# Loading routing probabilities chunk by chunk, and a small DMA in place of matmuls for the total decay

## The chip, the cores and the metric

The kernel runs on one core of one Trainium2 chip. The metric is the device time of one execution in microseconds (us). Three timed runs of the kernel before gave 314.59, 313.70 and 313.29 us, a median of 313.7 us. The engines of the core are PE (matmuls; PEld is its weight loads), DVE, ACT, POOL and SP. SP computes nothing here: it issues the DMAs, one after the other, each once what it waits for is there. POOL also issues DMAs, those of the expert weights.

## The reference

Two stages follow one another. The first is a gated recurrence for each batch and head (4 batches, 8 heads, 768 steps, head width 48), the second a mixture of 4 experts on the recurrence's output, seen as 3072 rows of 384.

```python
f = 1.0 / (1.0 + np.exp(-f_logit))
for t in range(S):
    state = f[:, :, t, :, None] * state + np.einsum('bhd,bhe->bhde', k[:, :, t], v[:, :, t])
    y[:, :, t] = np.einsum('bhd,bhde->bhe', q[:, :, t], state)
...
p = domain_probs / (domain_probs.sum(-1, keepdims=True) + 1e-09)
for e in range(E):
    h = np.maximum(x @ w1[e], 0.0)
    out += p[:, e:e + 1] * (h @ w2[e])
```

## The kernel before, in words

**Chunks.** The 768 steps are cut into 6 chunks c of 128 steps, which lie on the partitions. For each chunk and batch b the attention part works as follows. `gate1` and `gate2` (ACT, L240 and L244) turn the gate logits into -log f, called gp. `pe_cs` (PE) sums gp over the steps with a triangular matrix Ub (L248); four further matmuls (L251), one for each pair of heads, multiply gp by a column of ones, which gives the sum over the whole chunk, already on the partitions of the state (channel d of head 2i at partition d, of head 2i+1 at partition 64+d). `exps` (ACT) makes e[:,0] = exp(-sum) and e[:,1] = exp(sum) (L255, L256) and, from the four columns, egs, the total decay of the chunk (L258). `product` (L261, POOL or DVE) multiplies q by e[:,0] and k by e[:,1]. In chunks 0 and 1 PE transposes the products (L269) and ACT or DVE copies them out; from chunk 2 on a DMA does it (`dma_tp`, L273). `pe_at`, `ev_at` and `pe_y` (L284, L288, L295, L299) make the chunk's output; its transposed copy xT comes from PE in chunks 0 and 1 and from a DMA (`dma_xt`, L277) afterwards. `pe_kv`, `ev_kv` and `state` (L305, L312, L319, L320) bring the state forward: state, on POOL, multiplies it by egs and makes a bf16 copy for the next chunk. The last chunk has no state step, and so no egs.

**Experts.** For each chunk and expert e, `mm_h` (L328) multiplies xT by w1 in 8 groups of 3 matmuls; `relu` moves them out of PSUM (ACT L336, DVE L334). `mm_o` (L340) multiplies by w2, two groups of 4 matmuls for each batch nt; `ev_o` scales the result by the probability pn and adds it up in a tile o (expert 0: ACT L349 or DVE L351; experts 1 to 3: DVE L347). `store` (L355) writes o out. The relu of a later expert and the ev_o of an earlier one share ACT and DVE, each of which works in its own fixed order. PSUM has 4 banks for these results (`ps_m`), and PE can't begin a group before a bank is free.

**The probabilities.** One DMA on SP (L370) loads all 3072 rows of 4 probabilities into pt, 128 partitions by 24 columns by 4, behind the 16 loads of chunk 0. `probs` (DVE, L234 to L237) normalizes all of them once, into pn. Every `ev_o` depends on it.

**What sets the order.** A planner in the kernel, class `Plan`, gives every step a cost on the engines that may run it, a priority, what it depends on, and rooms (buffers) that it takes and frees. It plays the program through and puts the steps down in the order in which they would start; the instructions of each engine stand in that order and are waited for in that order. On SP too: a DMA whose source isn't ready holds up all those behind it. The planner's costs only set the order; the times in this document are from the chip. The weights come by 8 DMAs on POOL's queue (L229), and SP's first load of chunk 1 (f, L222) is made to wait until the sixth of them has landed. The tile e has 2 rooms, o has 8.

**Warming up.** Before the first expert matmul the program fills PE's gaps with matmuls on a tile called busy (L533).

Of the kernel before, what the change touches and what calls it, by code (L numbers as in the profile page):

```python
# [10 lines left out]
AF = mybir.ActivationFunctionType  # L11
ALU = mybir.AluOpType
# [87 lines left out]
def kernel(  # L100
# [14 lines left out]
    T = 128  # L115
# [17 lines left out]
    ps = ctx.enter_context(tc.tile_pool(name="ps", bufs=1, space=PS))  # L133
    rooms = {"ps_m": 4, "ps_t": 4, "f": 4, "q": 4, "k": 4, "v": 4, "ex": 2, "gp": 4, "e": 2, "qk": 7,
             "vb": 7, "egs": 8, "QK": 2, "AT": 2, "yb": 2, "xT": 2, "h": 2, "o": 8}
    P = Plan(rooms)
# [95 lines left out]

    def probs(eng):
        nc.vector.tensor_reduce(out=psm, in_=pt, axis=mybir.AxisListType.X, op=ALU.add)  # L234
        nc.vector.tensor_single_scalar(out=psm, in_=psm, scalar=1e-9, op=ALU.add)
        nc.vector.reciprocal(out=psm, in_=psm)  # L236
        nc.vector.tensor_tensor(out=pn, in0=pt, in1=psm.broadcast_to([128, B * C, E]), op=ALU.mult)  # L237

# [7 lines left out]
    def pe_cs(c, b):  # L246
        g, cs = tl("gp", c, b // 2)[:, b % 2], tl("cs", c, b)
        nc.tensor.matmul(out=cs[:, 0:HD], lhsT=Ub, rhs=g[:, :, 0:D], start=True, stop=True)  # L248
        if c < C - 1:
            for i in range(NP):  # L250
                nc.tensor.matmul(out=cs[0:MP, HD + i:HD + i + 1], lhsT=flat(g, i)[:, 0:MP], rhs=ones, start=True, stop=True)  # L251

    def exps(c, b):
        cs, e = tl("cs", c, b), tl("e", c, b)
        nc.scalar.activation(out=e[:, 0], in_=cs[:, 0:HD], func=AF.Exp, scale=-1.0)  # L255
        nc.scalar.activation(out=e[:, 1], in_=cs[:, 0:HD], func=AF.Exp)  # L256
        if c < C - 1:
            nc.scalar.activation(out=tl("egs", c, b), in_=cs[0:MP, HD:HD + NP], func=AF.Exp, scale=-1.0)  # L258

    def product(c, b, j, eng):  # L260
        engines[eng].tensor_tensor(out=tl("qk", c, b)[:, j, :, 0:D], in0=tl("qk"[j], c, b // 2)[:, hh(b), :],  # L261
                                   in1=tl("e", c, b)[:, j].rearrange("t (h d) -> t h d", d=D), op=ALU.mult)

# [104 lines left out]
    for i, x in enumerate("f0 k0 q0 f1 k1 q1 f2 f3 k2 q2 v0 k3 q3 v1 v2 v3".split()):  # L368
        add_load(0, x[0], int(x[1]), 1, -1000 + i)
    pload = P.add("ld p", {"DMA": 0.3}, lambda e: nc.sync.dma_start(  # L370
        out=pt, in_=moe_domain_probs.rearrange("(n p) e -> p n e", p=128)), -900, lag=2.0)
    wd = {}
# [11 lines left out]
    def attention(c, slot, gran):  # L384
        G, X, Y = {}, [], []
        more = c < C - 1
# [8 lines left out]
        for b in range(B):  # L395
# [4 lines left out]
            one = lambda f, *x: (lambda e, b=b: f(c, b, *x, e))  # L400
            cs = P.add(f"cs {c}.{b}", {"PE": 0.36 if more else 0.17}, on(pe_cs), s(0),
                       deps=[G[b]], takes=[pt_("cs")], lag=0.2, frees=[("gp", c, half)])
            ex = P.add(f"exps {c}.{b}", {"ACT": 1.1}, on(exps), s(0) + 0.1, deps=[cs],
                       takes=[("e", c, b)] + ([("egs", c, b)] if more else []), frees=[pt_("cs")])
            pe = {"DVE": 0.6, "POOL": 1.0} if c < 2 else {"POOL": 1.0}
# [61 lines left out]
    def add_o(c, e, nt, half):  # L467
# [5 lines left out]
        if half == 1:  # L473
            ev = oev[c, e, nt] = P.add(f"ev_o {c}.{e}.{nt}", {"ACT": 0.58, "DVE": 0.56} if e == 0 else {"DVE": 0.62},
                                       lambda g: ev_o(c, e, nt, g), p - 1, deps=[m, oev.get((c, e - 1, nt)), pdone],
                                       takes=[("o", c, nt)], frees=[key])
# [4 lines left out]
    pdone = P.add("probs", {"DVE": 1.2}, probs, 3, deps=[pload, xdone[0, B - 1]])  # L481
    ALL, LO, HI = list(range(B)), [0, 1], [2, 3]
# [13 lines left out]
    def ol(c, e, nts):  # L496
        return [(c, e, nt, half) for nt in nts for half in range(2)]

    for c in range(C):
        u0 = unit[0]  # L500
        if c == 0:
            zip_units(hl(c, 0, 0, NT, ALL), [])
# [65 lines left out]
```

## Time and profile before

| what | value |
|---|---|
| median of three timed runs | 313.7 us (313.29 to 314.59) |
| the profiled execution, its own time | 314.51 us |
| its span, first to last instruction | 312.8 us |
| PE busy | 297.2 us, 95% of the span |
| ACT busy | 164.8 us, 53% |
| DVE busy | 133.0 us, 43% |
| POOL busy | 90.0 us, 29% |
| mean granted clock of PE | 0.987 |
| the load of the probabilities, issue to landing | 23.5 us |

The span is 1.7 us shorter than that execution's own time. Rows of a timeline read: start, length (both us), engine, line, operation, out<-in, count, and in brackets how long the engine sat idle before it and who ended that. Rows of the waits read: who waited <- for whom: total us, times, longest. Rows by windows give for each stretch the busy time of each engine with its number of instructions, then PE's granted clock and the DMA engines' share. A time behind a line's number is in us from the start of the span.

### The profile page before, as it was taken

Reading aid. Unit: us, or ns where it says so; the run is one execution under the profiler, and the core shown is the slowest. Engines: PE = TensorE matmul, PEld = TensorE weight load, DVE = VectorE, ACT = ScalarE, POOL = GpSimd, SP = SyncE. Lnnn points to the kernel's source line nnn. Section 1 sums busy time; section 2 is a strip of 40 time slices with the busy share of each in tenths; the row PEclk is TensorE's granted clock in tenths of the full one; section 3 lists DMA queues with packets and bytes.
Section 4 is the critical chain, followed back from the end, with each engine's and each line's share of the span. In section 5 each row is a group of like instructions: output and inputs, shape, how many; then the busy total and the mean of one; then the engine's idle time right before and its main releaser. Section 6 shows DMA issues by size and latency. Waiting matters only on the chain.

```text
span 312.8 us, 5558 instructions
## 1 busy us (share of the span) xinstructions
PE 297.2 (95%) x2168; PEld 172.7 (55%) x2199; DVE 133.0 (43%) x250; ACT 164.8 (53%) x314; POOL 90.0 (29%) x156
## 2 busy tenths in 40 slices
PE   6889589999999999999999999999999999999995
PEld 5654235567786565555555555555555555555552
DVE  5750041378964754443755232653332452201223
ACT  5758055565875645566535466434466444465430
POOL 4470070036196441232533322523322200000000
PEclk9999969999999999999999999999999999999999
DMA  8999999998827589897987322200322200200002
GB/s 157 210 185 203 206 203 198 206 219 150 170 59 136 100 170 221 188 198 141 190 169 142 105 65 46 48 13 15 109 63 46 47 15 13 78 25 0 2 0 101
DMA packets 135082, 36.06 MB, mean 115 GB/s; under 512 B 126352, under 2 KB 133520, under 8 KB 135056
## 3 DMA queue, kind: packets, MB, share of 16 engines
q1 hardware_dynamic: 129296, 29.42, 48.4%
q0 software_dynamic: 5760, 6.29, 12.0%
q8 instruction: 17, 0.28, 0.4%
q14 instruction: 9, 0.07, 0.1%
HBM read 31.51 MB, written 4.72 MB: 116 GB/s over the span
## 4 chain that ended last, share of the span: by engine, by line
PE 85%; DMA 8%; SPq 4%; issue 1%; DVE 1%; ACT 0%; ACTq 0%
PE ps_m L340 40%; PE ps_m L328 37%; DMA pt<-in_moe_domain_probs_dram 8%; SPq L222 4%; PE ps_t L284 2%; PE ps_t L299 1%; PE ps_t L295 1%; PE ps_t L305 1%; PE ps_t L248 1%; PE ps_t L251 1%; PE ps_t L269 1%; DVE o L347 0%; PE ps_t L324 0%; ACT o L349 0%; DVE psm L236 0%
## 5 line engine op out<-in xcount | busy, mean ns | idle before, releaser
L328 PE MATMUL ps_m<-xT,w_sb 128*128 128x512 bf16 (+1 forms) x593 | 152.5, 364 | 6.6 <-ACT o L349 5.0
L336 ACT ACTIVATE h<-ps_m 128x512 bf16<-128x512 f32 (+1 forms) x173 | 99.5, 575 | 110.5 <-PE ps_m L328 101.7
L340 PE MATMUL ps_m<-w_sb,h 128*128 128x384 bf16 x768 | 155.2, 328 | 0.5 <-DMA w_sb<-in_moe_w_dram 0.3
L340 PEld LDWEIGHTS <-h 128*128 128x128 bf16 x768 | 72.3, 98 | 58.2 <-issue 1.8
L328 PEld LDWEIGHTS <-w_sb 128*128 128x128 bf16 x624 | 60.2, 98 | 51.2 <-issue 6.2
L347 DVE SCALAR_TENSOR_TENSOR o<-ps_m,pn,o 128x384 f32<-128x384 f32 x72 | 44.5, 618 | 98.0 <-PE ps_m L340 94.6
L319 POOL TENSOR_TENSOR Sf<-Sf,egs 48x192 f32<-48x192 f32 x40 | 20.1, 502 | 71.6 <-DVE Sf L312 69.8
L288 DVE TENSOR_TENSOR AT<-ps_t,mask 128x512 bf16<-128x512 f32 x48 | 31.1, 685 | 13.1 <-PE ps_t L284 12.8
L261 POOL TENSOR_TENSOR qk<-q,e 128x384 bf16<-128x384 f32 x18 | 18.2, 1017 | 55.4 <-ACT e L255 53.0
L334 DVE TENSOR_SCALAR h<-ps_m 128x512 bf16<-128x512 f32 (+1 forms) x35 | 20.0, 583 | 23.2 <-PE ps_m L328 22.8
L261 POOL TENSOR_TENSOR qk<-k,e 128x384 bf16<-128x384 f32 x20 | 20.7, 1033 | 6.8 <-ACT egs L258 6.7
L312 DVE TENSOR_TENSOR Sf<-Sf,ps_t 48x192 f32<-48x192 f32 x40 | 14.0, 350 | 12.5 <-PE ps_t L305 11.6
L349 ACT ACTIVATE o<-ps_m,pn 128x384 f32<-128x384 f32 x22 | 12.7, 581 | 11.8 <-DVE pn L237 7.8
L320 POOL CAST sb<-Sf 48x192 bf16<-48x192 f32 x40 | 13.6, 339 | 2.6
L255 ACT ACTIVATE e<-ps_t 128x384 f32<-128x384 f32 x24 | 11.7, 489 | 4.9 <-PE ps_t L251 4.5
L218 POOL CAST vb<-v 128x384 bf16<-128x384 f32 x18 | 9.5, 542 | 15.9 <-PE ps_t L305 7.9
L533 PE MATMUL ps_m<-busy 128*128 128x256 bf16 x71 | 11.5, 301 | 1.3 <-DVE busy L140 1.3
L256 ACT ACTIVATE e<-ps_t 128x384 f32<-128x384 f32 x24 | 11.9, 494 | 0.0
L240 ACT ACTIVATE ex<-f 128x768 f32<-128x768 f32 (+1 forms) x14 | 10.5, 752 | 2.4 <-DMA f<-in_f_logit_dram 2.2
L299 PE MATMUL ps_t<-vb,AT 128*128 128x48 bf16 x192 | 11.4, 184 | 0.0
L218 DVE CAST yb<-ps_t 128x384 bf16<-128x384 f32 x15 | 8.3, 556 | 6.9 <-PE ps_t L299 6.0
L299 PEld LDWEIGHTS <-AT 128*128 128x128 bf16 x192 | 9.9, 97 | 1.9
(50 smaller groups left out, 148.9 us busy)
## 6 DMA issues: line engine op xcount, KB each, us to landing
w_sb<-in_moe_w_dram POOLq DMA_DIRECT2D x8, 768.0 KB, 19.3
out_dram<-o SPq DMA_DIRECT2D x24, 192.0 KB, 1.9
f<-in_f_logit_dram SPq DMA_DIRECT2D x10, 384.0 KB, 5.0
k<-in_k_dram SPq DMA_DIRECT2D x10, 384.0 KB, 5.5
q<-in_q_dram SPq DMA_DIRECT2D x10, 384.0 KB, 5.0
v<-in_v_dram SPq DMA_DIRECT2D x10, 384.0 KB, 5.4
f<-in_f_logit_dram SPq DMA_DIRECT2D x4, 192.0 KB, 3.8
k<-in_k_dram SPq DMA_DIRECT2D x4, 192.0 KB, 4.0
```

The costliest lines, as they stand in the source:

```text
L218: engines[eng].tensor_copy(out=out, in_=in_)
L261: engines[eng].tensor_tensor(out=tl("qk", c, b)[:, j, :, 0:D], in0=tl("qk"[j], c, b // 2)[:, hh(b), :], in1=tl("e", c, b)[:, j].rearrange( ...
L288: nc.vector.tensor_tensor(out=tl("AT", c, b)[:, r].rearrange("s i t -> s (i t)"), in0=tl("A", c, b, r).rearrange("s i t -> s (i t)"), in1= ...
L299: nc.tensor.matmul(out=y[:, h * D:(h + 1) * D], lhsT=AT[:, r, i, :], rhs=vb[:, h, :], start=(c == 0), stop=True, skip_group_check=True)
L312: nc.vector.tensor_tensor(out=Sf[rows, b], in0=Sf[rows, b], in1=KV[rows, :, r, :], op=ALU.add)
L319: nc.gpsimd.tensor_tensor(out=Sf[rows, b], in0=Sf[rows, b], in1=eg, op=ALU.mult)
L320: nc.gpsimd.tensor_copy(out=nb[rows, b, :, r * D:(r + 1) * D], in_=Sf[rows, b])
L328: nc.tensor.matmul(out=tl("hp", c, e, fc, n0)[:, n0:n1], lhsT=w1_sb[:, e, kk, fc * 128:(fc + 1) * 128], rhs=tl("xT", c)[:, kk, n0:n1], sta ...
L334: nc.vector.tensor_relu(out=dst, in_=src)
L336: nc.scalar.activation(out=dst, in_=src, func=AF.Relu)
L340: nc.tensor.matmul(out=tl("op", c, e, nt)[:, 0:Din], lhsT=tl("h", c, e)[:, fc, nt * T:(nt + 1) * T], rhs=w2_sb[:, e, fc, :], start=(fc == ...
L347: nc.vector.scalar_tensor_tensor(out=o, in0=op, scalar=pe, in1=o, op0=ALU.mult, op1=ALU.add)
```

## The change

Three things change together.

The probabilities are loaded in six DMAs of 512 rows, one for each chunk, and normalized in six steps `probs c`. The first load stands on SP where the single one stood; those of later chunks are spread over the program. An `ev_o` of chunk c now waits for `probs c`.

The four matmuls with the column of ones and the third exponential are left to chunk 0. From chunk 1 to 4 the total decay is taken from exp's last row: e[:,0] at step 127 of the chunk is exp(-sum over the chunk) for all channels, and two DMAs on SP (`dma_egs`) carry its 384 numbers from one partition to the 2 x 48 partitions of egs, 48 pieces of 16 bytes each. `state` waits for them. For the pieces to be contiguous, e[:,0] is written in another layout, (d, r, i) in place of (i, r, d), head h = 2i + r: ACT writes, and the product of q reads, neighbouring channels of a head 32 bytes apart. The layout is used in all six chunks.

The rooms change: e from 2 to 3, since it is now held until the DMA has read it, and o from 8 to 6. The planner's costs follow, so that its order changes in places.

```diff
-    rooms = {... "e": 2, ... "o": 8}
+    rooms = {... "e": 3, ... "o": 6}
...
+    p_src = moe_domain_probs.rearrange("(b c p) e -> p b c e", p=128, c=C)
+    p_dst = pt.rearrange("p (b c) e -> p b c e", c=C)
+    def load_p(c):
+        nc.sync.dma_start(out=p_dst[:, :, c], in_=p_src[:, :, c])
...
-        if c < C - 1:
+        if c == 0:
             for i in range(NP):
                 nc.tensor.matmul(out=cs[0:MP, HD + i:HD + i + 1], lhsT=flat(g, i)[:, 0:MP], rhs=ones, start=True, stop=True)
...
-        nc.scalar.activation(out=e[:, 0], in_=cs[:, 0:HD], func=AF.Exp, scale=-1.0)
+        nc.scalar.activation(out=e[:, 0].rearrange("t (d h) -> t h d", d=D), in_=cs[:, 0:HD].rearrange("t (i r d) -> t r i d", r=2, d=D),
+                             func=AF.Exp, scale=-1.0)
         nc.scalar.activation(out=e[:, 1], in_=cs[:, 0:HD], func=AF.Exp)
-        if c < C - 1:
+        if c == 0:
             nc.scalar.activation(out=tl("egs", c, b), in_=cs[0:MP, HD:HD + NP], func=AF.Exp, scale=-1.0)
+    def dma_egs(c, b):
+        last = tl("e", c, b)[T - 1:T, 0].rearrange("o (d r i) -> o r d i", r=2, d=D)
+        for r in range(2):
+            nc.sync.dma_start(out=tl("egs", c, b)[r * P2:r * P2 + D, :], in_=last[:, r])
...
+            GS.append(P.add(f"egs {c}.{b}", {"DMA": 1.0}, on(dma_egs), s(3), deps=[ex], takes=[("egs", c, b)],
+                            frees=[("e", c, b)], lag=2.0) if c and more else None)
...
-                                 deps=[ek], frees=[("egs", c, b)])
+                                 deps=[ek, GS[b]], frees=[("egs", c, b)])
...
+        pl = P.add(f"ld p{c}", {"DMA": 0.5}, lambda e, c=c: load_p(c), -900 if c == 0 else u0 - 6, lag=2.0)
+        pdone.append(P.add(f"probs {c}", {"DVE": 0.8}, lambda e, c=c: probs(c), u0 + 4, deps=[pl, xdone[c, B - 1]]))
```

Line numbers of the changed kernel differ: L237 is the load of probabilities, L255 the sum with Ub, L262 and L264 the two exponentials, L271 the DMAs of egs, L276 the product, L344 mm_h, L356 mm_o.

SP, behind the loads of chunk 0 (the numbers are buffers). Before:

```order
L222 DMA q_204<-in_q_dram 128x8x48
L222 DMA v_229<-in_v_dram 128x8x48
L222 DMA v_315<-in_v_dram 128x8x48 x2
L370 DMA pt<-in_moe_domain_probs_dram 128x24x4
L222 DMA f_698<-in_f_logit_dram 128x16x48
```

And in the changed kernel:

```order
L222 DMA q_204<-in_q_dram 128x8x48
L222 DMA v_229<-in_v_dram 128x8x48
L222 DMA v_315<-in_v_dram 128x8x48 x2
L237 DMA pt<-in_moe_domain_probs_dram 128x4x4
L222 DMA f_699<-in_f_logit_dram 128x16x48
```

Only the size of the load has changed at this place: 4 columns of 4 numbers for each partition in place of 24.

SP, behind the loads of chunk 1. Before, the loads of chunk 2 follow at once:

```order
L222 DMA k_897<-in_k_dram 128x16x48
L222 DMA q_929<-in_q_dram 128x16x48
L222 DMA v_970<-in_v_dram 128x16x48
L222 DMA f_1010<-in_f_logit_dram 128x16x48
L222 DMA k_1045<-in_k_dram 128x16x48
L222 DMA q_1089<-in_q_dram 128x16x48
```

And in the changed kernel:

```order
L222 DMA k_885<-in_k_dram 128x16x48
L222 DMA q_926<-in_q_dram 128x16x48
L222 DMA v_960<-in_v_dram 128x16x48
L271 DMA egs_986<-e_774 48x1x4 x2
L271 DMA egs_1000<-e_783 48x1x4 x2
L271 DMA egs_1025<-e_972 48x1x4 x2
L237 DMA pt<-in_moe_domain_probs_dram 128x4x4
L271 DMA egs_1061<-e_1008 48x1x4 x2
L222 DMA f_1086<-in_f_logit_dram 128x16x48
```

Nine issues have moved in between, eight of which wait for exponentials of chunk 1, and the loads of chunk 2 stand behind them.

PE, the two sums of batches 0 and 1 of chunk 1 (gp_90), among the matmuls of the experts. Before:

```order
L328 MATMUL ps_m_755<-xT_342,w_sb 128x512
L248 LDWEIGHTS Ub
L248 MATMUL ps_t_761<-gp_90,Ub 128x384
L251 LDWEIGHTS gp_90
L251 MATMUL ps_t_761<-ones,gp_90 112x1
...
L248 LDWEIGHTS Ub
L248 MATMUL ps_t_767<-gp_90,Ub 128x384
L251 LDWEIGHTS gp_90
L251 MATMUL ps_t_767<-ones,gp_90 112x1
...
L340 LDWEIGHTS h_642
```

And in the changed kernel:

```order
L344 MATMUL ps_m_755<-xT_342,w_sb 128x512
L255 LDWEIGHTS Ub
L255 MATMUL ps_t_761<-gp_90,Ub 128x384
L255 LDWEIGHTS Ub
L255 MATMUL ps_t_763<-gp_90,Ub 128x384
L356 LDWEIGHTS h_642
```

The sums stand between the same expert matmuls as before, without the four L251 behind each.

More of the change, by code (lines that the diff above doesn't have):

```diff
@@ L133 @@
     ps = ctx.enter_context(tc.tile_pool(name="ps", bufs=1, space=PS))
-    rooms = {"ps_m": 4, "ps_t": 4, "f": 4, "q": 4, "k": 4, "v": 4, "ex": 2, "gp": 4, "e": 2, "qk": 7,
-             "vb": 7, "egs": 8, "QK": 2, "AT": 2, "yb": 2, "xT": 2, "h": 2, "o": 8}
+    rooms = {"ps_m": 4, "ps_t": 4, "f": 4, "q": 4, "k": 4, "v": 4, "ex": 2, "gp": 4, "e": 3, "qk": 7,
+             "vb": 7, "egs": 8, "QK": 2, "AT": 2, "yb": 2, "xT": 2, "h": 2, "o": 6}
     P = Plan(rooms)
@@ L369 @@
         add_load(0, x[0], int(x[1]), 1, -1000 + i)
-    pload = P.add("ld p", {"DMA": 0.3}, lambda e: nc.sync.dma_start(
-        out=pt, in_=moe_domain_probs.rearrange("(n p) e -> p n e", p=128)), -900, lag=2.0)
     wd = {}
```

30 lines of the change are left out of this document (17 added, 13 removed).

## The prediction

> **What bounds the kernel now.** I read the page first, then the list of waits, then the timeline around the one place where PE stands still. On the page:
>
> ```profile
> span 312.8 us, 5558 instructions
> ...
> PE 297.2 (95%) x2168; PEld 172.7 (55%) x2199; DVE 133.0 (43%) x250; ACT 164.8 (53%) x314; POOL 90.0 (29%) x156
> ...
> PEclk9999969999999999999999999999999999999999
> ```
>
> PE is busy for 95% of the span, so PE's work and its few gaps set the end. The clock row has one low digit, the sixth slice, 39.1 to 46.9 us (a slice is 312.8 / 40 = 7.82 us): something let PE go idle there. The waits, longest first in total, name it:
>
> ```profile
> DVE psm L234 <- DMA pt<-in_moe_domain_probs_dram: 17.3, 1, 17.3
> ACT o L349 <- DVE pn L237: 7.8, 1, 7.8
> PE ps_m L328 <- ACT o L349: 5.0, 1, 5.0
> ```
>
> Read from below: PE waited 5.0 us once for an ACT eviction, which waited for the normalized probabilities, which waited for the DMA of pt. The timeline gives the places:
>
> ```profile
> 14.89 0.81 SPq L370 DMA_DIRECT2D pt<-in_moe_domain_probs_dram  x1
> ...
> 38.45 0.25 DVE L234 TENSOR_REDUCE psm<-pt 128x24 f32<-128x96 f32 x1 [17.28 <-DMA pt<-in_moe_domain_probs_dram]
> ...
> 39.64 1.05 ACT L349 ACTIVATE o<-ps_m,pn 128x384 f32<-128x384 f32 x2 [7.85 <-DVE pn L237]
> ...
> 40.27 1.44 PE L328 MATMUL ps_m<-xT,w_sb 128*128 128x512 bf16 x3 [4.96 <-ACT o L349]
> ```
>
> What the stall costs, I read from PE's busy time by stretches (busy time and instructions of PE first, the granted clock behind POOL):
>
> ```profile
> 35.30:40.27 4.97, 0.01 (x1) 0.00 (x0) 1.66 (x7) 0.63 (x2) 0.39 (x1) 0.81 1.32 209
> 40.27:45.28 5.01, 5.01 (x14) 2.08 (x14) 2.06 (x6) 2.68 (x5) 4.30 (x11) 0.51 1.27 203
> 45.28:50.00 4.72, 4.67 (x26) 2.46 (x26) 0.00 (x0) 2.96 (x5) 2.04 (x6) 1.00 1.27 190
> ```
>
> After the gap the clock is 0.51 for 5.01 us, in which 14 matmuls pass; at full clock 26 pass in 4.67 us, so these 14 would take 14 x 4.67 / 26 = 2.5 us. The stall costs 4.96 us of idle time and 5.01 - 2.5 = 2.5 us of slow clock, 7.5 us together.
>
> **The change: the load of probabilities.** One DMA of 3072 pieces of 16 bytes landed 23.5 us after its issue (14.89 to 38.4). The first of the new ones has a sixth of the pieces. Its landing isn't in the trace; if time goes by pieces it is 23.5 / 6 = 3.9 us, about 19 us on the clock of the trace; if it shares the queues with the weights as badly as the load of f below, which took 10.1 us, it is 25. It is needed when ACT first asked, 39.64 - 7.85 = 31.8 us. Both ends are in time, so I take the 7.5 us as gone. The normalization is split in six; one took from 38.45 to 39.64 with its handovers, 1.2 us, so the five new ones cost DVE at most 6 us, on an engine busy 43%.
>
> **The matmuls with ones.** In chunk 1 the sums of two batches stand thus on PE:
>
> ```profile
> 61.50 0.33 PE L248 MATMUL ps_t<-gp,Ub 128*128 128x384 bf16 x1
> 61.66 0.32 PE L251 MATMUL ps_t<-ones,gp 128*112 128x1 bf16 x4
> 61.85 0.32 PE L248 MATMUL ps_t<-gp,Ub 128*128 128x384 bf16 x1
> 62.01 0.32 PE L251 MATMUL ps_t<-ones,gp 128*112 128x1 bf16 x4
> 62.19 0.81 PE L340 MATMUL ps_m<-w_sb,h 128*128 128x384 bf16 x4
> ```
>
> Durations overlap in the pipeline, so I price by starts: the four cost 61.85 - 61.66 = 0.19 and 62.19 - 62.01 = 0.18 us. They go in chunks 1 to 4, 16 groups: 16 x 0.185 = 3.0 us, all on PE, which is the bound there. The 16 third exponentials go from ACT, which isn't.
>
> **What is late next.** With the stall gone, PE comes 7.5 us earlier to chunk 1, while the loads of chunk 1 don't move: SP issues f when the sixth weight has landed.
>
> ```profile
> 42.72 0.37 SPq L222 DMA_DIRECT2D f<-in_f_logit_dram  x1
> f<-in_f_logit_dram SPq DMA_DIRECT2D x1, 384.0 KB, 10.1
> 58.36 0.83 ACT L240 ACTIVATE ex<-f 128x768 f32<-128x768 f32 x1
> 59.23 0.84 ACT L244 ACTIVATE gp<-ex 128x768 bf16<-128x768 f32 x1
> ```
>
> (The second row is that load's time to landing.) It lands at 42.72 + 10.1 = 52.8; the gate began at 58.36, with 5.5 us to spare, and would now begin at 50.9. So ACT will wait up to 1.9 us for f, and behind it on ACT stand gate2, the relus of expert 3 and the exponentials, for which PE waits in turn. PE itself reaches the sum at 61.50 - 7.5 = 54.0; f plus both gates gives 52.8 + 0.83 + 0.84 = 54.5 and a handover. The cost lies between 0.6 and 1.9 us; I take 0.8, since relus ahead keep PE supplied for a while.
>
> **The new layout.** ACT now writes e[:,0], and the product of q reads it, 32 bytes apart. The rows for today's layout:
>
> ```profile
> L255 ACT ACTIVATE e<-ps_t 128x384 f32<-128x384 f32 x24 | 11.7, 489 | 4.9 <-PE ps_t L251 4.5 <-POOL qk L261 0.4
> L261 POOL TENSOR_TENSOR qk<-q,e 128x384 bf16<-128x384 f32 x18 | 18.2, 1017 | 55.4 <-ACT e L255 53.0 <-ACT e L256 2.0
> ```
>
> No row of this kernel reads or writes single elements that far apart, so I bound it by nothing and by a doubling: 0.49 us more for each exponential and 1.0 for each product on POOL, 1.5 us in a batch. What hides it: from chunk 2 on a transposed product lands well before PE wants it; in the batch with the least room that I found,
>
> ```profile
> 102.43 1.24 SPq L273 DMA_TRANSPOSE QK<-qk  x1
> QK<-qk SPq DMA_TRANSPOSE x1, 3.2
> 107.66 0.40 PE L284 MATMUL ps_t<-QK 48*128 48x128 bf16 x8
> ```
>
> it lands at 102.43 + 3.2 = 105.6 and is used at 107.66, 2.1 us later, more than 1.5. Chunk 0 has less cover:
>
> ```profile
> 21.61 0.48 ACT L216 COPY xT<-ps_t 128x384 bf16<-128x384 bf16 x1 [0.71 <-PE ps_t L324]
> 22.42 1.47 PE L328 MATMUL ps_m<-xT,w_sb 128*128 128x512 bf16 x5 [0.31 <-DMA w_sb<-in_moe_w_dram]
> ```
>
> The last xT is ready at 22.1 and PE waits for the first weight until 22.4: 0.3 us of cover against four exponentials of 0.49, so up to 4 x 0.49 - 0.3 = 1.7 us. In chunk 1 PE transposes the products as soon as they are made; with its four batches working in pairs, up to 2 x 1.5 = 3 us, or 6 if nothing of a pair overlaps. So the layout costs 0 to 4.7 us, at worst 7.7. I take 0.9, a fifth of 4.7, nearer to nothing, because only one operand of each of these instructions is strided; the others stay as they are.
>
> A rule speaks against that. The Trainium skill, GPSIMD Engine Reference, section 7 (Performance pitfalls for Q7 kernels), says that reading SBUF with a step of more than 8 bytes costs about half as much again per element; no row here shows it. By it the product on POOL would go from 1.02 to about 1.5 us, an estimate, and two exposed pairs in chunk 1 would add 1.0 us to the sum, in place of my 0.9 for all engines, which leaves the forecast where it is.
>
> **The DMAs of egs.** They add 32 issues on SP, and 5 more for the probabilities. `state` on POOL waits long anyway, and SP's own waits are for work that isn't done yet:
>
> ```profile
> POOL Sf L319 <- DVE Sf L312: 69.8, 13, 18.5
> SPq L355 <- DVE o L347: 79.7, 20, 32.7
> out_dram<-o SPq DMA_DIRECT2D x24, 192.0 KB, 1.9
> ```
>
> A DMA of a similar kind lands 1.9 us after its issue, so egs comes some 2 us after the exponentials, when the products have just been made; I cost it at nothing. What stands behind them on SP: the loads of chunk 2, the transposes and the stores. The tile o with 6 rooms in place of 8 needs a store to land (1.9 us) before the third tile of the next chunk is begun; its first user comes a whole expert later, so nothing. For all that the new order may misplace, DVE's five normalizations among it, I put 0.3 us.
>
> **The sum.** -4.96 - 2.5 - 3.0 + 0.8 + 0.9 + 0.3 = -8.5 us. The profiled execution, 314.51 us by its own time (span 312.8 and 1.7 around it), would take 306.0; it is 0.8 above the median of the three runs, 313.7. Against that median the forecast is 305.2 us.
>
> **The rivals.**
>
> *The layout costs a full doubling.* For it: strided access is what the edit introduces, and chunks 0 and 1 have nearly no cover; the rule above points this way too. Against it: only q's side is strided, and from chunk 2 on 2.1 us of room swallow it. Price: 4.7 to 7.7 in place of 0.9, so 309.0 to 312.0. Chance 0.12.
>
> *The stall stays.* The first DMA would have to land after 31.8, which is 17 us after its issue, for a sixth of the pieces; that is so only if its time is made by the weights on the other queue and not by its own pieces. Then only the 3.0 us of matmuls are gained, less 0.9 for the layout: 311.6. The load of f landed in 10.1 us beside the same weights with more pieces and 48 times the bytes, which speaks against it. Chance 0.04.
>
> *Slower: SP becomes the bound.* It works its list in order, and every copy xT of chunks 2 to 5 stands behind egs issues that wait for exponentials. The tightest place today, at the start of chunk 4's expert work:
>
> ```profile
> 212.62 1.18 SPq L277 DMA_TRANSPOSE xT<-yb  x1
> xT<-yb SPq DMA_TRANSPOSE x1, 3.5
> 216.58 0.81 PE L328 MATMUL ps_m<-xT,w_sb 128*128 128x512 bf16 x3
> ```
>
> It lands at 216.1 and PE starts at 216.6: 0.5 us of room. There are 8 egs issues to a chunk. At 0.4 us each, as a load's issue above, SP idles long enough to take them. If each held SP for 1.2 us like a transpose, and SP had no idle time, xT would come 9 us late at each of four chunk starts, 36 us in all: 341. The kernel is slower than before once the four starts lose more than 8.5 + 1.6 = 10.1 us together, 2.5 us at each beyond the room. Against it stand SP's waits, 79.7 us in one row alone. If it happens, it is likely to be at a few places; I price it at 3.5 us each, 305.2 + 14 = 319. Chance 0.04.
>
> **How the numbers follow.** The forecast, 305.2 us, has 0.80 (with the layout between 0 and a third of the doubling). Without any of the three new costs it would be 313.7 - 10.5 = 303.2; with f at 1.9 and the layout's 4.7 it is 310.1. The range from 303.2 to 309.4 holds the forecast's case and the lower part of the first rival, and leaves out the other rivals. About 0.5%, 1.6 us, is what a measurement of this kernel can tell from no change: faster below 312.1, slower above 315.3. Faster is then the forecast, the first rival and the second, less a little for the upper ends: 0.93. Within 0.5%: 0.03. Slower: the third rival, 0.04.
>
> **What would show it.** In the changed profile the clock row has no low digit, the wait of DVE for pt is short, and no wait of PE for ACT L349's successor stands in the list. PE has 64 matmuls fewer. A wait of ACT's gate for f of chunk 1 is new, 1 to 2 us. The rows of the exponential into e[:,0] and of q's products say what the layout costs: 489 and 1017 ns if nothing. The forecast is wrong if PE waits for xT at the chunk starts, or if the gap around 35 us is still there.

## The result, and the profile after

The changed kernel takes 305.1 us (median of 4 runs, 305.03 to 305.37). The kernel before took 313.5 us (median of 4 runs, the three known before among them, 311.93 to 314.59). The ratio is 0.974, with a 95% interval of 0.970 to 0.978. Some executions of the experiments below were longer at a lower granted clock (one of the kernel before took 511.42 us at 0.559); their medians, ranges and ratios leave these out.

The page of the changed kernel, whose profiled execution took 305.37 us by its own time:

```profile
span 303.5 us, 5499 instructions
...
PE 294.5 (97%) x2104; PEld 170.5 (56%) x2135; DVE 137.8 (45%) x272; ACT 170.7 (56%) x295; POOL 95.7 (32%) x157
...
PEclk9999999999999999999999999999999999999999
```

PE has 64 instructions fewer (2168 to 2104), and the low digit of the clock row is gone. All waits of PE of 0.3 us or more:

```profile
PE ps_m L551 <- DVE busy L140: 1.3, 1, 1.3
PE ps_t L315 <- DVE vb L218: 0.7, 1, 0.7
PE ps_t L255 <- ACT gp L251: 0.4, 1, 0.4
PE ps_m L344 <- DVE o L367: 0.3, 1, 0.3
PE ps_t L285 <- DVE qk L276: 0.3, 1, 0.3
```

The 5.0 us for ACT's eviction stand no more in the list. By their places in the timeline the first three rows lie ahead of the first expert matmul; only the last two, 0.6 us together, come behind it (at 81.9 and 70.5 us). The timeline shows the load that used to be late, the normalization of chunk 0, the first expert matmul, the gate of chunk 1 and the two sums behind it:

```profile
14.97 0.68 SPq L237 DMA_DIRECT2D pt<-in_moe_domain_probs_dram  x1
...
22.42 0.17 DVE L241 TENSOR_REDUCE psm<-pt 128x4 f32<-128x16 f32 x1 [0.41 <-DMA pt<-in_moe_domain_probs_dram]
...
23.04 1.47 PE L344 MATMUL ps_m<-xT,w_sb 128*128 128x512 bf16 x5
...
52.66 0.84 ACT L247 ACTIVATE ex<-f 128x768 f32<-128x768 f32 x1 [1.38 <-DMA f<-in_f_logit_dram]
...
54.43 0.48 PE L255 MATMUL ps_t<-gp,Ub 128*128 128x384 bf16 x2
```

DVE waits 0.41 us for the probabilities in place of 17.28. ACT's gate waits 1.38 us for f. The sums begin at 54.43, where the prediction had 54.0 without and 54.5 with that wait; no idle time of PE stands in front of them.

Where did the time go? I split the span at the first expert matmul (22.42 before, 23.04 after). Busy time of PE by stretches, the kernel before:

```profile
22.42:312.80 290.38, 279.56 (x1969) 159.99 (x2000) 117.61 (x215) 150.86 (x284) 77.33 (x133) 0.99 0.57 110
...
45.00:90.00 45.00, 44.84 (x392) 29.47 (x394) 26.61 (x50) 27.73 (x59) 15.09 (x27) 1.00 0.95 172
```

The changed kernel:

```profile
23.04:303.50 280.46, 274.60 (x1905) 156.04 (x1936) 120.91 (x234) 155.75 (x265) 82.08 (x134) 1.00 0.59 114
...
45.00:90.00 45.00, 44.22 (x387) 29.82 (x388) 30.54 (x61) 30.62 (x55) 18.82 (x28) 1.00 0.96 170
```

From the first expert matmul to the end it takes 290.38 - 280.46 = 9.92 us less. Half of that is busy time of PE, 279.56 - 274.60 = 4.96 us: the slow clock and the matmuls with ones. The other half is idle time, (290.38 - 279.56) - (280.46 - 274.60) = 4.96 us, as long as the gap. The three terms of the prediction (4.96, 2.5, 3.0) make 10.46; the gap is right, and the other two are 0.5 us too large together. Between 45 and 90 us PE stands still for 0.78 us in place of 0.16, 0.62 more, where chunk 1's attention and the start of chunk 2's lie; elsewhere it stands still for about as much less, half of that behind its last matmul. The start is 0.62 us later, and 9.92 - 0.62 = 9.3 is the difference of the spans.

What the new layout costs where it is used:

```profile
L276 POOL TENSOR_TENSOR qk<-q,e 128x384 bf16<-128x384 f32 x19 | 22.8, 1203 | 66.7 <-ACT e L262 66.2
...
L262 ACT ACTIVATE e<-ps_t 128x384 f32<-128x384 f32 x24 | 20.7, 864 | 4.6 <-PE ps_t L255 2.4
...
L264 ACT ACTIVATE e<-ps_t 128x384 f32<-128x384 f32 x24 | 13.0, 541 | 0.0
```

ACT's strided exponential went from 489 to 864 ns, 77% more; POOL's product of q from 1017 to 1203 ns, 18% more. What keeps its layout moved less: the second exponential went from 494 to 541 ns, POOL's product of k from 1033 to 1064.

And SP's list behind the loads of chunk 1, in the changed kernel:

```profile
60.75 8.74 SPq L271 DMA_DIRECT2D egs<-e  x6
...
70.42 1.14 SPq L271 DMA_DIRECT2D egs<-e  x2
71.60 0.59 SPq L222 DMA_DIRECT2D f<-in_f_logit_dram  x1
```

Before, the same load of chunk 2 (f) came straight behind those of chunk 1:

```profile
61.89 1.67 SPq L222 DMA_DIRECT2D f<-in_f_logit_dram  x1
```

It is issued 9.7 us later now. In the changed kernel it lands 3.9 us after its issue, at 75.5, and the gate that uses it begins at 77.88:

```profile
77.88 0.84 ACT L247 ACTIVATE ex<-f 128x768 f32<-128x768 f32 x1
```

Nothing waits for it yet, with 2.4 us to spare. Before, it landed after 5.6 us, at 67.5, 13 us ahead of its gate at 80.74. This is what the later experiments turn on.

### The profile page after: what moved, and what is told of

It reads as the page before. It is cut to its first block, busy times and chain, and to the rows that moved or that the text cites. A ratio compares the mean times of both kernels' runs of the same rounds, so it can differ in the third digit from the quotient of the medians.

```text
span 303.5 us, 5499 instructions
## 1 busy us (share of the span) xinstructions
PE 294.5 (97%) x2104; PEld 170.5 (56%) x2135; DVE 137.8 (45%) x272; ACT 170.7 (56%) x295; POOL 95.7 (32%) x157
## 4 chain that ended last, share of the span: by engine, by line
PE 90%; DMA 4%; DVE 2%; POOL 1%; issue 1%; ACT 1%; DVEq 0%; ACTq 0%; POOLq 0%
PE ps_m L356 40%; PE ps_m L344 40%; DMA w_sb<-in_moe_w_dram 3%; PE ps_t L300 2%; PE ps_t L255 1%; PE ps_t L315 1%; PE ps_t L321 1%; PE ps_t L311 1%; PE ps_t L285 1%; DMA f<-in_f_logit_dram 1%; POOL qk L276 1%; PE ps_m L551 1%; DVE qk L276 1%; DVE o L363 0%; DVE AT L304 0%
## 5 line engine op out<-in xcount | busy, mean ns | idle before, releaser
L352 ACT ACTIVATE h<-ps_m 128x512 bf16<-128x512 f32 (+1 forms) x171 | 98.4, 578 | 102.7 <-PE ps_m L344 92.5
L356 PE MATMUL ps_m<-w_sb,h 128*128 128x384 bf16 x768 | 153.0, 326 | 0.2
L344 PE MATMUL ps_m<-xT,w_sb 128*128 128x512 bf16 (+1 forms) x593 | 150.4, 362 | 1.9 <-DVE o L367 0.3
L356 PEld LDWEIGHTS <-h 128*128 128x128 bf16 x768 | 72.5, 98 | 57.4
L344 PEld LDWEIGHTS <-w_sb 128*128 128x128 bf16 x624 | 59.8, 98 | 46.9 <-issue 0.7
L276 POOL TENSOR_TENSOR qk<-q,e 128x384 bf16<-128x384 f32 x19 | 22.8, 1203 | 66.7 <-ACT e L262 66.2
L350 DVE TENSOR_SCALAR h<-ps_m 128x512 bf16<-128x512 f32 (+1 forms) x37 | 20.7, 573 | 22.0 <-PE ps_m L344 19.7
L276 POOL TENSOR_TENSOR qk<-k,e 128x384 bf16<-128x384 f32 x20 | 21.3, 1064 | 20.3 <-ACT e L264 13.0
L262 ACT ACTIVATE e<-ps_t 128x384 f32<-128x384 f32 x24 | 20.7, 864 | 4.6 <-PE ps_t L255 2.4
L551 PE MATMUL ps_m<-busy 128*128 128x256 bf16 x71 | 13.1, 332 | 1.3 <-DVE busy L140 1.3
L365 ACT ACTIVATE o<-ps_m,pn 128x384 f32<-128x384 f32 x20 | 11.6, 581 | 3.9 <-PE ps_m L356 3.1
L264 ACT ACTIVATE e<-ps_t 128x384 f32<-128x384 f32 x24 | 13.0, 541 | 0.0
L251 ACT ACTIVATE gp<-ex 128x768 bf16<-128x768 f32 (+1 forms) x14 | 10.5, 751 | 0.4
```

Of the source, the lines that this page charges most:

```text
L262: nc.scalar.activation(out=e[:, 0].rearrange("t (d h) -> t h d", d=D), in_=cs[:, 0:HD].rearrange("t (i r d) -> t r i d", r=2, d=D), func=A ...
L276: engines[eng].tensor_tensor(out=tl("qk", c, b)[:, j, :, 0:D].rearrange("t (i r) d -> t i r d", r=2), in0=tl("qk"[j], c, b // 2)[:, hh(b), ...
L344: nc.tensor.matmul(out=tl("hp", c, e, fc, n0)[:, n0:n1], lhsT=w1_sb[:, e, kk, fc * 128:(fc + 1) * 128], rhs=tl("xT", c)[:, kk, n0:n1], sta ...
L350: nc.vector.tensor_relu(out=dst, in_=src)
L352: nc.scalar.activation(out=dst, in_=src, func=AF.Relu)
L356: nc.tensor.matmul(out=tl("op", c, e, nt)[:, 0:Din], lhsT=tl("h", c, e)[:, fc, nt * T:(nt + 1) * T], rhs=w2_sb[:, e, fc, :], start=(fc == ...
```

## The experiments

My theory: the stall, the slow clock behind it and the matmuls with ones make the gain; the layout and the small DMAs lie beside other work. Rivals: the layout costs PE time; SP's list is at its edge; the stall would not have cost the clock. Line numbers shift by a few between kernels. The groups ran on different chips, so a ratio is always to the kernel before on the same chip. It took 313.6 us (310.15 to 314.79) beside `egs2`, `egs_pool` and `f_early`, and 314.9 us (313.58 to 315.79) beside `egs_pool_e4`; beside the others its time is given there.

### The chunked load alone, and the small DMAs alone

`p_only` is the kernel before with the six loads of probabilities; `egs_only` is the changed kernel with the single load.

```diff
 p_only, against the changed kernel:
-    rooms = {... "e": 3, ... "o": 6}
+    rooms = {... "e": 2, ... "o": 8}
-        if c == 0:
+        if c < C - 1:
             (four matmuls with ones; the third exponential; e[:,0] in the old layout)
-    def dma_egs(c, b): ...

 egs_only, against the changed kernel:
-        pl = P.add(f"ld p{c}", ... load_p(c) ...)
-        pdone.append(P.add(f"probs {c}", ...))
+    pload = P.add("ld p", ...)       (one DMA)
+    pdone = P.add("probs", ...)      (one normalization)
```

> The kernel before with the chunked load and normalization alone; the matmuls with ones, the layout of e and the rooms stay as before. If the two parts are independent, the stall's 7.5 us go and the 3.0 us of matmuls stay, while the new layout's cost (0.6 us at the start of the changed kernel) does not come: 305.1 + 3.0 - 0.6 = 307.5, between 306.8 and 308.2. If the matmuls with ones were hidden after all, so that all of the gain is the stall, it is 305.1 or a little less. The clock row has no low digit in either case.

> The changed kernel with the single load of all probabilities put back, and nothing else. If the parts are independent, the gap at 35 us and the slow clock behind it are back: the load lands near 38.4 again, PE comes to its last step before the gap some 0.3 us later than before, so 7.2 us are lost and the wait for f of chunk 1 disappears: 305.1 + 7.2 - 0.4 = 311.9, between 311.0 and 312.6. If egs and the layout brought nothing, it is the time of before, 313.5.

The kernel before took 314.5 us on this chip (312.6 to 316.9). `p_only` took 309.2 us (308.9 to 310.8), ratio 0.985, interval 0.975 to 0.996. `egs_only` took 311.2 us (310.3 to 312.2), ratio 0.989, interval 0.983 to 0.996. Each half gains; neither comes near the 0.974 of both. `egs_only` lies within what I expected, `p_only` 1 us above it. In `p_only` the stall is gone, but PE stands still for 1.4 us between 45 and 90 us, nearly all of it at one place:

```profile
83.56 3.11 PE L335 MATMUL ps_m<-xT,w_sb 128*128 128x256 bf16 x27 [1.18 <-DVE o L358]
...
45.00:90.00 45.00, 43.57 (x403) 30.05 (x404) 30.13 (x60) 28.83 (x64) 18.59 (x30) 1.00 0.99 188
```

(The second row is from the stretches.) PE waits there for a bank of PSUM that DVE empties late. The changed kernel has the same wait with 0.35 us, at 81.9. `p_only` has neither the new layout nor the small DMAs, and waits longer; so this wait needs neither of them. That PE now arrives earlier at a busy DVE is the likely reason, though the order of DVE's work differs too. From its first expert matmul to the end of its span:

```profile
23.26:307.10 283.84, 277.33 (x1969) 159.18 (x1999) 119.48 (x233) 152.47 (x286) 77.32 (x133) 1.00 0.56 112
```

That is 3.4 us more than the 280.46 of the changed kernel: 277.33 - 274.60 = 2.73 us of PE's busy time and 0.65 of idle time. The 2.73 us are the price of the 16 groups with ones; the prediction had 3.0. Against the kernel before, with the same 1969 matmuls, the busy time is 279.56 - 277.33 = 2.2 us less, which is the price of the slow clock there. `p_only` missed its range by that idle time, and because I had taken the later start for a cost of the layout: without that layout it still begins at 23.26.

In `egs_only` the old gap is back at its old length:

```profile
39.26 0.25 DVE L234 TENSOR_REDUCE psm<-pt 128x24 f32<-128x96 f32 x1 [17.52 <-DMA pt<-in_moe_domain_probs_dram]
...
41.08 1.44 PE L337 MATMUL ps_m<-xT,w_sb 128*128 128x512 bf16 x3 [4.99 <-ACT o L358]
...
41.00:44.40 3.40, 3.32 (x9) 1.28 (x9) 2.11 (x7) 2.15 (x5) 2.91 (x8) 0.51 1.26 201
```

(The third row is from the stretches, with the granted clock third from the right.) The clock behind it is low for 3.4 us and not for the 5.0 us that PE spent at 0.51 in the kernel before. From the first expert matmul (23.47) to the end PE is busy for 275.82 us, 1.2 more than the changed kernel with as many matmuls. So a gap of the same length cost 2.2 us of slow clock in one execution and 1.2 in the other.

### The first load of probabilities held back

Does the stall cost the clock too, and from what length of gap? `late2` and `late4` hold the first small load until the third, or the fifth, weight has landed.

```diff
     def load_p(c):
-        nc.sync.dma_start(out=p_dst[:, :, c], in_=p_src[:, :, c])
+        x = nc.sync.dma_start(out=p_dst[:, :, c], in_=p_src[:, :, c])
+        if c == 0:
+            after(x, ins["w", 2])      # late4: ins["w", 4]
...
+    (the step "ld p0" is put down behind the issue of that weight)
```

> The changed kernel, but the first load of probabilities is issued only when the third weight has landed (30.9 us in the changed kernel's trace). With some 5 us to its own landing, it lands near 36, ACT evicts near 37, and PE waits about 1 us. A gap that short should leave the clock alone, so 305.1 + 1 = 306.1 at most. If the load takes only the 2.8 us that the later ones took, it lands at 33.7 and costs nothing.

> The same, held until the fifth weight has landed (38.5 us). It lands near 43.5, PE stands from about 36.6 to 45, 8.5 us, and finds a half clock that costs 2.5 us more; the later wait for f is swallowed, -0.4: 305.1 + 10.6 = 315.7. If the gap cost only its own length, 313.2. If the load lands in 2.8 us, 2 us less in both.

One run each, so tenths say little: `late2` 309.07 us, `late4` 316.55 us, against 305.37 of the changed kernel's profiled run. In `late4` the gap is 8.92 us:

```profile
46.83 1.44 PE L346 MATMUL ps_m<-xT,w_sb 128*128 128x512 bf16 x3 [8.92 <-ACT o L367]
```

The granted clock by stretches (the third number from the right), `late4`:

```profile
42.60:46.00 3.40, 0.00 (x0) 0.00 (x0) 0.59 (x4) 0.00 (x0) 0.00 (x0) 0.51 1.49 201
46.00:49.40 3.40, 2.57 (x8) 1.06 (x8) 2.83 (x9) 2.61 (x5) 2.52 (x7) 0.50 1.27 189
```

The same in `late2`, whose gap is only 2.10 us (it ends at 38.72):

```profile
35.60:39.00 3.40, 1.30 (x8) 0.64 (x7) 1.64 (x7) 0.91 (x2) 0.59 (x2) 1.00 1.30 211
39.00:42.40 3.40, 3.40 (x11) 1.40 (x10) 1.78 (x6) 1.58 (x4) 2.90 (x8) 0.50 1.20 204
42.40:45.80 3.40, 3.35 (x19) 1.71 (x18) 0.00 (x0) 2.96 (x5) 2.91 (x8) 0.99 1.32 204
```

And in the kernel before, whose gap ran from 35.30 to 40.27:

```profile
35.00:38.40 3.40, 0.32 (x2) 0.09 (x1) 0.00 (x0) 0.00 (x0) 0.00 (x0) 1.00 1.45 206
38.40:41.80 3.40, 1.53 (x4) 0.56 (x4) 3.06 (x11) 1.59 (x4) 1.68 (x4) 0.50 1.15 208
41.80:45.20 3.40, 3.40 (x11) 1.52 (x10) 0.66 (x2) 1.72 (x3) 2.93 (x7) 0.50 1.32 204
```

So a gap does cost the clock, and a gap of 2.1 us is enough. I had expected that the short one would leave the clock alone; that fell. The low clock comes in steps of 3.4 us: one step in `late2`, behind a stretch in which PE was busy for 1.30 of 3.40 us, two in the kernel before and in `late4`. In a step at half clock about 11 instructions pass instead of 19, so a whole one costs 3.4 x 8 / 19 = 1.4 us. The Trainium skill, TensorE: Matmul & The Clock Gate, Part 1, describes a free-running window of about 3.4 us and half the clock after an idle one; the steps agree. Its table "Why this matters for your kernels" asks only for no gaps above some 3 us; `late2` shows that a shorter one can do it, when all of it falls into one such stretch (35.6 to 39.0 us). Stretches in which PE was busy for 1.30 (`late2`) and 1.53 us (before) of 3.40 were followed by a slow one; one with 2.11 in `late4` (35.8 to 39.2 us) and one with 1.90 in `egs_only` (34.2 to 37.6 us) were not.

This nearly closes both sums. `late2`: a gap of 2.1 and a step of 1.4 us, less a start 0.34 us earlier (22.70), make 3.2 of its 3.7 us. `late4`: 8.92 of gap, 1.3 in the part of the second step in which matmuls ran (2.57 us at half clock), and a start 0.94 us later (its first expert matmul is at 23.98) make 11.2, and the run is 11.2 us longer. The clock is confirmed, but 2.5 us was the price in one run: it depends on how many slow steps follow a gap, and on how much of them falls into the gap itself.

### The old layout in chunk 0, and the old way in chunks 0 and 1

```diff
 chunk0:
-        nc.scalar.activation(out=e[:, 0].rearrange(...), ...)
+        if c == 0:          # old01: if c < 2
+            nc.scalar.activation(out=e[:, 0], in_=cs[:, 0:HD], func=AF.Exp, scale=-1.0)
+        else:
+            nc.scalar.activation(out=e[:, 0].rearrange(...), ...)
 old01, besides:
-        if c == 0:
+        if c < 2:
             (four matmuls with ones; the third exponential; no small DMAs in chunk 1)
```

> The changed kernel with the old contiguous layout of e[:,0] in chunk 0 alone, where no DMA reads it. If the layout is what makes the first expert matmul start at 23.04 instead of 22.42, it starts at 22.4 again and the kernel takes 304.5. If that delay comes from the first weight's landing alone, by chance of that run, the start stays at 23.0 and the time at 305.1.

> The changed kernel with the matmuls with ones, the third exponential and the contiguous layout kept in chunks 0 and 1, the two in which PE transposes products and nothing covers the layout; DMAs for egs only in chunks 2 to 4. PE gets 4 groups of 0.185 back, 0.74 us; the start's 0.6 us is saved, and whatever the layout costs in chunk 1: at my 0.3 to 0.5 us there, 305.1 + 0.74 - 0.6 - 0.4 = 304.8. If chunk 1 costs nothing, 305.2; if it costs 2 us, 303.2.

The kernel before took 313.7 us beside them (313.4 to 314.0). `chunk0`: 305.3 us (305.03 to 305.50), ratio 0.973, interval 0.972 to 0.974: no gain, though ACT is 0.375 us faster at each of the four exponentials of chunk 0. So the second case of its expectation holds: the layout doesn't make the start. In `chunk0` what ends the start is the first weight, as PE's row shows:

```profile
22.65 1.47 PE L347 MATMUL ps_m<-xT,w_sb 128*128 128x512 bf16 x6 [0.27 <-DMA w_sb<-in_moe_w_dram]
```

In the changed kernel it is PE's weight load (PEld) that waits for the same weight, 0.36 us, until 23.03. Through the profiles that row lies between 22.42 and 23.98 us, whatever the layout; only in that of `egs_pool_e4`, below, does it come at 29.47, behind a late load of v.

`old01`: 306.8 us (306.4 to 307.35), ratio 0.978, interval 0.977 to 0.979. That is 1.5 us slower than `chunk0` on the same chip, although it spares chunk 1 the strided layout as well. Between 45 and 90 us its PE waits for these:

```profile
PE ps_m L347 <- DVE o L370: 0.7, 1, 0.7
PE ps_m L347 <- DVE h L353: 0.3, 1, 0.3
PE ps_t L255 <- ACT gp L251: 0.2, 1, 0.2
```

These are 1.2 us, against 0.7 in `chunk0` (`o` 0.4, a product 0.3). The four groups with ones that it keeps are 4 x 0.185 = 0.7 us. Together 1.2 of the 1.5. I had expected 303.2 to 305.2, and that fell: the old way costs more in chunk 1 than the new one. The run doesn't price the layout there by itself, since the order of the program moves with it.

### More small DMAs on SP

Three kernels load SP's list: `egs2` issues each pair of small DMAs once more into a tile that nobody reads (64 issues in place of 32), `egs4` three times more (128), and `contig8` has the old layout in all chunks and carries the decay in 8 DMAs for each batch, of 4-byte pieces (128).

```diff
 egs2, egs4:
         for r in range(2):
             nc.sync.dma_start(out=tl("egs", c, b)[r * P2:r * P2 + D, :], in_=last[:, r])
+        for i in range(3):          # egs2: once
+            for r in range(2):
+                nc.sync.dma_start(out=more_egs[i][r * P2:r * P2 + D, :], in_=last[:, r])
 contig8:
+        for i in range(NP):
+            for r in range(2):
+                nc.sync.dma_start(out=tl("egs", c, b)[r * P2:r * P2 + D, i:i + 1],
+                                  in_=tl("e", c, b)[T - 1:T, 0, (2 * i + r) * D:(2 * i + r + 1) * D])
```

> The changed kernel with six further DMAs of the same kind into scratch tiles behind each pair for egs, 96 more issues on SP of about 0.55 us each, 13 us for each of chunks 1 to 4. If SP's waits cover them, as I hold, the time stays within 0.5 us of 305.1. If SP is close to being the bound (the third rival of the prediction), the copies xT, which land 1.3 to 2.9 us ahead of use at the chunk starts, come late: several us more, 310 or above.

> The changed kernel with e[:,0] in the old contiguous layout in all chunks, so that exponentials and products cost what they did before; egs then comes in eight DMAs of 48 pieces of 4 bytes for each batch instead of two of 16 bytes. SP issues as much as in the kernel with six more DMAs. If the layout costs about 1 us in all, as in the prediction's sum, and SP has room, 304.1. If the layout is hidden except for the start, 304.5. If SP is the bound, 310 or above in both kernels.

> The changed kernel with one more pair of small DMAs behind each pair that carries the total decay, into a tile that nobody reads: 64 such issues on SP in place of 32 (with 128 the kernel took 359 us). Where between 32 and 128 does SP become the bound? At 0.58 us an issue the 8 further issues of a chunk add 4.6 us to SP's list, and the 32 of the changed kernel already moved the first load of chunk 2 from 61.89 to 71.60 us. If the changed kernel still has 4.6 us of room at the tightest place: 305.1 +- 0.5 us. If it stands at the edge: SP's further 4.6 us show in part at each of four chunk starts, 308 to 324 us, with PE waiting for a transposed product or for f of chunk 2. I expect 308 to 315, since the f of chunk 2 landed only about 2 us ahead of its gate.

| small DMAs on SP | kernel | us | ratio to before, interval |
|---|---|---|---|
| 32 | changed | 305.1 | 0.974 (0.970 to 0.978) |
| 64 | `egs2` | 317.3 (315.7 to 318.6) | 1.013 (1.006 to 1.019) |
| 128 | `contig8` | 355.5 (354.2 to 356.7) | 1.133 (1.130 to 1.136) |
| 128 | `egs4` | 359.1 (358.9 to 360.3) | 1.146 (1.143 to 1.148) |

For `egs4` I had expected no change, since SP's waits would take the further issues. That fell altogether. PE's waits in `egs4`:

```profile
PE ps_t L304 <- DMA QK<-qk: 26.9, 9, 7.2
PE ps_m L348 <- ACT h L356: 10.9, 1, 10.9
```

The transposed products and, through ACT, the gates come late: the transposes and loads stand on SP behind issues that wait for exponentials, and SP takes 0.6 us for each issue even when it waits for nothing. With 64 issues the same begins, and it takes more than the 308 to 315 us that I had expected:

```profile
PE ps_t L303 <- DMA QK<-qk: 5.6, 4, 2.2
PE ps_m L347 <- ACT h L355: 1.9, 1, 1.9
```

SP's list in `egs2` where the loads of chunk 2 begin:

```profile
73.85 1.14 SPq L272 DMA_DIRECT2D egs<-e  x2
75.03 1.22 SPq L274 DMA_DIRECT2D more<-e  x2
76.30 0.58 SPq L223 DMA_DIRECT2D f<-in_f_logit_dram  x1
```

The f of chunk 2 is issued at 76.30, 4.7 us later than in the changed kernel, which is more than the 2.4 us that it had to spare. It lands after 5.6 us, and ACT's gate waits for it:

```profile
81.92 0.84 ACT L248 ACTIVATE ex<-f 128x768 f32<-128x768 f32 x1 [2.93 <-DMA f<-in_f_logit_dram]
```

Of the 12.1 us by which the span of `egs2` is longer (315.6 against 303.5), 8.3 are idle time of PE; the other 3.8 are longer busy time for the same 2104 instructions, at a mean granted clock of 0.989 in place of 1.000. The changed kernel is therefore within one such delay of the case of the third rival of the prediction. `contig8` is 3.6 us faster than `egs4` with the same number of issues; its exponential is back at 488 ns. With SP as the bound in both, and with other pieces in the DMAs, that is no price of the layout in the changed kernel.

### The small DMAs issued by POOL, and a fourth room for e

```diff
 egs_pool:
-            nc.sync.dma_start(out=tl("egs", c, b)[...], in_=last[:, r])
+            nc.gpsimd.dma_start(out=tl("egs", c, b)[...], in_=last[:, r])
 egs_pool_e4, besides:
-    rooms = {... "e": 3, ...}
+    rooms = {... "e": 4, ...}
```

> The changed kernel with the 32 small DMAs of the total decay issued by POOL in place of SP, at the same places of the order; they compute the same. SP then has the list of the kernel before but for the five loads of probabilities. If SP's list limits the changed kernel anywhere (PE had 0.7 us of waits between 70 and 90 us, and the loads of chunk 2 came 10 us later than before), this is faster, 303.5 to 304.5 us, and the first load of chunk 2 is issued near 62 us again. If SP's list costs nothing at 32 issues: 305.1 +- 0.5 us. If POOL, which now waits for the exponentials ahead of products and states and spends about 0.9 us on an issue, becomes late: 307 us or more, with PE waiting for products that POOL makes. I expect 305.1 +- 0.5.

> The run before this with the small DMAs of the total decay on POOL, and with 4 rooms for the tile e in place of 3; the planner's order follows in places. There PE lost 3.1 us at 75.7 us of the span waiting for a copied product of chunk 1, ACT's exponential of the fourth batch had waited 4.1 us for a DMA of egs to have read e, and the clock was lower behind it (0.91 between 70 and 90 us). If the held room of e is the cause, both waits go with it and the clock stays at 1.0: 310.1 - 3.1 - 1.0 to 2.0 = 305.0 to 306.0 us, and less (304 to 305) if a free list on SP, with the first load of chunk 2 near 71 us, is worth something. If POOL's time for the issues is the cause (0.53 us each, ahead of the products), the wait stays: 308 us or more. I expect 305.0 to 306.0.

`egs_pool`: 310.1 us (308.5 to 311.3), ratio 0.990, interval 0.983 to 0.996, so slower than the changed kernel, where I had expected the same time. Its timeline in chunk 1:

```profile
69.52 3.08 POOL L271 DMA_DIRECT2D egs<-e  x6
...
73.62 0.86 ACT L262 ACTIVATE e<-ps_t 128x384 f32<-128x384 f32 x1 [4.13 <-DMA egs<-e]
...
75.74 0.40 PE L300 MATMUL ps_t<-QK 48*128 48x128 bf16 x8 [3.11 <-ACT QK L216]
```

POOL comes to the six issues only at 69.5, behind a product that had waited 9.2 us for an exponential (SP had begun at 60.75). Until they have read it, the three rooms of e are held; ACT's fourth exponential waits 4.1 us for one, and PE 3.1 us in turn, with a lower clock behind it (0.91 from 70 to 90 us). With four rooms that wait should go. The profiled execution of `egs_pool_e4` took 313.27 us: ACT waited 6.6 us for a load of v in chunk 0, and the first expert matmul came at 29.47, 6.5 us later than in `egs_pool`, so its stages lie that much later too. The wait did go: no wait of ACT for egs and none of PE for a copied product stands in its lists, and PE from 70 to 90 us, which holds the place at some 82 us, reads:

```profile
70.00:90.00 20.00, 19.23 (x209) 14.07 (x206) 16.18 (x35) 13.56 (x26) 12.95 (x25) 1.00 0.68 134
```

(16.14 of 20 in `egs_pool`.) The kernel takes 306.9 us (305.6 to 307.7), ratio 0.976, interval 0.973 to 0.979, which can't be told from the changed kernel's 0.974. Its f of chunk 2 is issued at 63.77, straight behind the loads of chunk 1 again, and yet the kernel isn't faster than the changed one: a free list on SP shows no gain. Since POOL now spends its own time on the issues, this is no clean price of SP's list with 32 issues. I had expected 305 to 306; what the last microsecond is, this run doesn't tell.

### The load of f released earlier

```diff
         if (c, nm, b) == (1, "f", 0):
-            after(ins[c, nm, b], ins["w", 5])
+            after(ins[c, nm, b], ins["w", 4])
```

> The changed kernel with the first load of chunk 1 (f) released by the fifth weight instead of the sixth, so some 4 us earlier. It tests the term of 0.8 us in the sum for ACT's gate of chunk 1, which waited 1.4 us for f in the changed kernel. If that wait costs PE what was taken, 304.3 us; if the relus ahead cover it altogether, 305.1 +- 0.3 us. A rival: f now takes transfer time from the weights, so that a later weight is late for PE: 305.5 us or more. I expect 304.7 to 305.1.

305.8 us (305.3 to 306.5), ratio 0.977, interval 0.970 to 0.983: no gain. The load's time to landing, in `f_early`:

```profile
f<-in_f_logit_dram SPq DMA_DIRECT2D x1, 384.0 KB, 14.7
```

and in the changed kernel:

```profile
f<-in_f_logit_dram SPq DMA_DIRECT2D x1, 384.0 KB, 10.4
```

It was issued at 39.13 in place of 42.25 and landed at 53.8 in place of 52.6. By the edit one more of the weights was still on its way, and the weights were slower as well: the slowest landed 32.7 us after its issue in place of 30.5. The run left the term of 0.8 us untested, since the wait it was to remove grew from 1.38 to 2.13 us; the rival in its expectation, contention, is what the two times to landing point to, with f itself late for ACT.

No version here beats the changed kernel.

## Why the prediction was right, point by point

**The stall and its clock.** Right: 4.96 us of gap are gone, and the clock is full. `egs_only`, which keeps the single load, keeps a gap of 4.99. The clock's 2.5 us, counted by matmuls, are 2.2 by PE's busy time, and they hold for that one profile: the gaps of `egs_only`, `late2` and `late4` cost 1.2 to 1.4 us of slow clock.

**The landing of the first small load.** Its size was off: 3.9 us by pieces was my estimate, 7.4 us was measured in the changed kernel:

```profile
pt<-in_moe_domain_probs_dram SPq DMA_DIRECT2D x1, 8.0 KB, 7.4
```

and 9.7 to 12.8 us in the nine other profiles that issue it at the same place. Those lie at the other bound, the 10.1 us of f, and beyond; where it was held back until a weight had landed, it took 6.3 (`late2`) and 6.2 us (`late4`). So the pieces don't make its time; what else is moving is the likely reason. It cost nothing, since it was needed only at 31.8.

**The matmuls with ones.** 3.0 us by starts, 2.7 us of PE's busy time between `p_only` and the changed kernel: the right kind, a little too large.

**What is late next.** The wait of ACT for f came as forecast, 1.38 us within 0.6 to 1.9, but PE lost nothing at the sums that its rows show, against the 0.8 that I took: the expert matmuls ahead of them lasted until gp was there. In `f_early`, where ACT waited 2.13 us, PE did wait, for 0.7 us:

```profile
55.61 0.48 PE L255 MATMUL ps_t<-gp,Ub 128*128 128x384 bf16 x2 [0.70 <-ACT gp L251]
```

So the cover was about 1.4 us, just enough: in the changed kernel the term of 0.8 us was worth nothing, and a somewhat longer wait costs PE time, as here.

**The layout.** Taken as 0.9 us for all; the single instructions cost more than I reckoned on ACT (0.375 us, three quarters of the doubling) and less on POOL (0.19 us). In time it shows as little: no gain from the old layout in chunk 0, and PE's only wait for a product of chunk 1 is 0.3 us. So the 0.9 us were too many, though no run prices the layout by itself. The rule of the Trainium skill against which I weighed it (GPSIMD Engine Reference, section 7) would give 1.5 us for the product on POOL, an estimate of half as much again; the row has 1.203, 18% more. Here the measurement decides.

**The DMAs of egs at nothing.** Right for the time, and wrong in its reason. I took 0.4 us an issue and let SP's idle time cover them; they take 0.57 (1.14 for two), and SP's idle time doesn't cover what stands behind a waiting issue. So the margin was thinner than I argued: 32 more issues make the kernel slower than before (1.013, interval 1.006 to 1.019).

**The start and the order.** 0.3 us was taken for the order. Of it PE's wait for DVE's evictions (0.35 us) is the measured part. 0.62 us came from a start that was later; since its place varies from profile to profile by more than that, I don't put it down to the change. The other number of rooms for o was not tested alone. The terms for what goes, 10.46 us, measured 9.92. Those for what comes, 2.0 us, measured 0.62 at the start and 0.16 outside the span; the 0.62 us of new idle time from 45 to 90 us were made up elsewhere. So the profiled execution gained 9.1 us where the sum had 8.5: both sides were taken too large, and the errors partly cancel. That the forecast of 305.2 meets the median of 305.1 is luck to that extent. The profiled execution came out 0.6 us below the 306.0 forecast for it, and it lies only 0.3 us above the median of its kernel, where the prediction took off 0.8.

## What to carry to other kernels

A small DMA in place of work on the bounding engine is cheap only while the in-order queue that issues it has lead to spare: look at what stands behind it, and how long before its use that is issued, not at how idle the queue is. When a stall goes, count the clock with it, and look for the next late load; in these runs gaps in PE of 2 to 9 us cost 1.2 to 2.2 us more in slow clock behind them. A tile that a DMA reads back is held until that DMA has run, so an issue that moves later needs another room.

## What was not expected of the hardware

- The low clock came in whole steps of 3.4 us, at 0.50 to 0.51, and one followed a gap of only 2.1 us. Gaps of 4.96 and 4.99 us brought two steps and one.
- ACT's exponential into elements 32 bytes apart took 864 ns in place of 489. POOL's product, with one operand strided, took 1203 in place of 1017.
- A DMA of 48 pieces of 16 bytes holds SP for 0.57 us and POOL for 0.53 us (16.6 us for 32).
- A load that was issued 3.1 us earlier, with one more weight still on its way, landed 1.2 us later.
